# Retention and two gated products in one kernel: stores, roundings and word buffers in other places

## The chip, the cores and the metric

The kernel runs on one core of one Trainium2 chip. The core's engines are TensorE (PE, with its weight loads as PEld), VectorE (DVE), ScalarE (ACT), GpSimd (POOL) and SyncE (SP), which here issues nearly all transfers. The metric is the device time of one execution in microseconds, and the median of several runs is compared.

## The reference

A retention layer with a decaying state per head is followed by two two-layer networks, the first with x·sigmoid(x) between its layers, the second with a leaky maximum. All is fp32.

```python
for t in range(S):                                  # S = 768, B = 2, H = 8, D = 64
    state = gamma * state + einsum('bhd,bhe->bhde', k[:, :, t], v[:, :, t])
    y[:, :, t] = scale * einsum('bhd,bhde->bhe', q[:, :, t], state)
x = y as 1536 tokens x 512
h = x @ moe_w_in;  x = (h / (1 + exp(-h))) @ moe_w_out        # 512 -> 2048 -> 512
h = x @ moe2_w_in; return maximum(0.01 * h, h) @ moe2_w_out
```

## The kernel before

**Stages.** Attention works on 12 chunks of 128 tokens (`ORDER`), two at a time: masked scores, values, a running state. Each network then has an up phase (512 to 2048, 8 steps of two 128-feature blocks, class `Step`) and a down phase (2048 to 512). The network products multiply a rounded high part and a remainder of each operand in three fp32r terms (`TERMS`), so every operand is first split by `halves`: ACT writes the high part, DVE subtracts to give the low part. From the third step on, the up phase uses a seven-product scheme for 2x2 blocks (`product`, `rest`), with the products in the order 6, 2, 5, 7, 1, 4, 3 of a step (6, 2, 7, 5, 4, 3 in the last), where product 1 is the next step's.

**Order.** The order of work is written by hand, engine by engine, and each engine runs its own list in order. In the up phase `tasks[m]` lists what goes to the other engines ahead of product m. SP's list is one queue for loads and stores alike.

**Weights.** A weight tile w arrives as 64-bit words in one of two `ws` tiles (`load_w`). `words` (ACT, L144 and L146) takes a buffer from the list `rt` and reads the words into it and into `u`; `clamp` (DVE, L150 and L154), `signed` (L161) and `low` (L168) finish the value. `keep_w` stores it to memory as `scr` and puts the buffer at the end of `rt`; `fetch_w` takes a buffer from `rt` and loads it again. For tiles of the second network's down phase `keep_s` also forms four sums of blocks (L181) and stores them as `scrs`.

**Features.** `Step.act` applies the nonlinearity in place on the step's 128x3072 tile (two tiles `big` in turn), and `Step.keep` stores the tile, 1.5 MB, as `g` (L445). The down phase fetches `g` in pieces (`fetch_g` L459, `Two.load` L510) and splits them (`split_g`; `Two.high` L555 and `Two.left` L559). Steps 0 to 5 are stored in the step that follows; step 6 is stored after the whole last step (L952), then step 7 (L955).

**Down phase of the second network** (class `Two`). Units n = 0 to 7 multiply the first 512 tokens plainly (L586), units from 8 on use seven products for 256 tokens each (L602). Ahead of unit n stand the splits of the weights for n + 2 (`third`, L200 and L201) and of the features for n + 2. In units 1 to 8 the sums of weights, loaded by `ask` (L576) into one of two hold tiles (`sf`, `u`), are rounded into `S[k]` (L648, L654); only units from 8 on read `S`.

**Attention's last part.** `store_x(j)` takes chunk j's outcome: for j below 6 DVE multiplies it by a decay (L363) into `xf` or `tm`, then `halves` writes the operands of the first network; from 6 on `halves` reads PSUM and ACT copies the raw value (L371). Chunks 3, 4 and 5 (counted from 0) are the second half of the first 768 tokens; their operands are `b12[0]` (a slot `w`) and `xb[0]`. `first_t` and `rest_t` form differences of `xf` and `tm` in place on POOL, from 49.47 us on.

Of the kernel before, what the change touches and what calls it, by code (L numbers as in the profile page):

```python
# [18 lines left out]
C = 128  # L19
# [11 lines left out]
PER = N // C  # L31
Q = NF // 2
WARM = 18
LATE = 6
PLACES = 6
NCST = NP * C + C + H + H + NP

MIN_NORMAL = float(np.array(0x38000000, np.uint32).view(np.float32))
# [4 lines left out]
def retention_moe_kernel(ctx: ExitStack, tc: tile.TileContext, att, w1, w2, cst, out):  # L43
# [93 lines left out]
            s = (w1, w2)[layer][f, :, 512 * part:512 * part + 512]  # L137
            nc.sync.dma_start(out=t[:, n], in_=s.bitcast(I32).rearrange("p (n t) -> p n t", t=2))

    def words(w, which=(0, 1)):  # L140
        t = stage[w]
        if 0 in which:
            r = rs[w] = rt.pop(0)
            nc.scalar.activation(out=r.bitcast(F32), in_=t[:, :, :, 1].bitcast(F32), func=AF.Abs)  # L144
        if 1 in which:
            nc.scalar.activation(out=u, in_=t[:, :, :, 0].bitcast(U32), func=AF.Copy, scale=2.0 ** -29)  # L146

    def clamp(w):
        r = rs[w]
        nc.vector.tensor_scalar(  # L150
            out=r.bitcast(F32), in0=r.bitcast(F32), scalar1=MIN_NORMAL, scalar2=MAX_NORMAL,
            op0=ALU.max, op1=ALU.min,
        )
        nc.vector.tensor_scalar(  # L154
            out=r, in0=r, scalar1=3, scalar2=0x3FFFFFF8,
            op0=ALU.logical_shift_left, op1=ALU.bitwise_and,
        )
# [8 lines left out]
    def low(w):  # L166
        r = rs[w]
        nc.vector.tensor_tensor(out=r, in0=r, in1=u, op=ALU.add)  # L168
# [186 lines left out]
    def store_x(j):  # L355
        s, c = divmod(j, PER)
        a, b = c * C, c * C + C
        y = yu[j]
        g4 = lambda t: t.rearrange("p (a k i) -> p a k i", a=2, k=2)
        y = g4(y)  # L360
        f = (tm if s % 2 else xf)[s // 2][:, :, :, a:b]
        if j < LATE:
            nc.vector.tensor_tensor(out=f, in0=y, in1=g4(G), op=ALU.mult)  # L363
            y = f
        if s % 2 == 0:
            halves(*(xa[s // 2][:, n].rearrange("p (a k) n -> p a k n", a=2)[:, :, :, a:b] for n in range(2)), y)
        else:
            halves(*put(s, a, b, 0)[0:2], y[:, 0])
            halves(*put(s, a, b, 1)[0:2], y[:, 1])
        if j >= LATE:  # L370
            nc.scalar.activation(out=f, in_=y, func=AF.Copy)  # L371


    TERMS = ((0, 0), (0, 1), (1, 0))
# [118 lines left out]
    class Two:  # L493
# [67 lines left out]
        def run(self):  # L561
# [65 lines left out]
            def third(i):  # L627
                return split_2((1, 1, i), wt[(i - 2) // 3][:, (i - 2) % 3])

            for n in range(self.UNITS):  # L630
                s, i = divmod(n, Q)
                if i == 0 and s % 2:
                    y = lanes_of(0)[0] + [bank(2), bank(3)]
                elif i == 0:
                    y = lanes_of(1)[0] + [bank(0), bank(1)]
                if n + 4 < 10:
                    self.fetch(n + 4)
                if n + 2 < Q:
                    third(n + 2)
                if n + 4 < Q:  # L640
                    fetch_w((1, 1, n + 4))
                if n >= 4 and n + 6 < self.UNITS:
                    self.fetch(n + 6)
                if n + 2 < self.UNITS:
                    self.high(n + 2)
                if 1 <= n <= Q:
                    k = n - 1
                    nc.scalar.activation(out=S[k][0], in_=hold[k % 2], func=AF.Copy)  # L648
                if Q <= n + 3 < self.UNITS:
                    self.sums(n + 3)  # L650
                if n + 2 < self.UNITS:
                    self.left(n + 2)
                if 1 <= n <= Q:
                    nc.vector.tensor_tensor(out=S[k][1], in0=hold[k % 2], in1=S[k][0].bitcast(F32), op=ALU.subtract)  # L654
                for k in range(2) if n == 0 else [n + 1] if n + 1 < Q else []:
                    ask(k)
                if s == 0:
                    plain(n, i, y)
                    if i == Q - 1:
                        for c in range(4):  # L660
                            nc.scalar.activation(
                                out=o[:, 2 * c:2 * c + 2].rearrange("p b n -> p (b n)"), in_=y[c], func=AF.Copy
                            )
                            send(c)
                else:
                    seven(n, i, y)
                    if i == Q - 1:
                        finish(s + 1, y)

    with tc.manual_schedule():  # L670
# [48 lines left out]
        def load_next():  # L719
            w = next(asked, None)  # L720
            if w is not None:
                load_w(w)

        def signed(w):
            sign(w)
            load_next()
# [15 lines left out]
        def left_a():  # L742
# [6 lines left out]
        amid = {2: lambda: words(wa), 4: low_a}  # L749
        behind = {  # L750
            0: load_next, 2: lambda: clamp(wa), 3: lambda: signed(wa),
            4: lambda: (load_next(), clamp(wb)), 5: lambda: signed(wb),
        }
        places = [place(p) for p in range(2)]
        for j in range(0, NJ, 2):
# [41 lines left out]
        def up_tasks(layer, k):  # L797
            t = [[] for _ in range(8)]
            at = lambda n, *f: t[n].extend(f)
            if layer == 0 and k < 2:  # L800
                wd = first_w[3]
                if k == 0:
                    at(0, lambda: low(wb), lambda: first_t(0, nc.gpsimd), lambda: rest_t(0, nc.gpsimd))
                    at(1, lambda: words(wc), lambda: split_a(wb))
                    at(2, lambda: clamp(wc), lambda: signed(wc))
                    at(3, lambda: low(wc), lambda: sums(wc))
                    at(4, lambda: split_t(0, 0), lambda: first_t(1, nc.vector))
                    at(6, lambda: split_t(1, 0))
                else:
                    at(0, lambda: split_t(0, 1), lambda: rest_t(1, nc.vector))  # L810
                    at(2, lambda: split_a(wc), lambda: words(wd))
                    at(3, lambda: split_s(wc))
                    at(4, lambda: split_t(1, 1), lambda: clamp(wd))
                    at(5, lambda: signed(wd))
                    at(6, lambda: low(wd), lambda: sums(wd))
                return t
            if layer == 0:
                if k + 1 < Q:
                    a = first_w[k + 1]
                    at(0, lambda: split_a(a))  # L820
                    at(1, lambda: split_s(a))
                w = second_w[0][k - 2]
                if k + 2 < Q:
                    b = first_w[k + 2]
                    at(0, lambda: words(b, (0,)))
                    at(2, lambda: words(b, (1,)), lambda: clamp(b))
                    at(3, lambda: signed(b))
                    at(4, lambda: (low(b), sums(b)), lambda: words(w, (0,)))
                    at(5, lambda: words(w, (1,)), lambda: clamp(w))
                    at(6, lambda: (signed(w), low(w), keep_w(w)))  # L830
                else:
                    at(1, lambda: words(w))
                    if k + 1 < Q:
                        at(2, lambda: clamp(w))
                        at(3, lambda: signed(w))
                    else:
                        at(4, lambda: clamp(w), lambda: signed(w))
                    at(4, lambda: low(w))
                    at(5 if k + 1 < Q else 4, lambda: direct(w))
                return t  # L840
            w = second_w[1][k]
            n, m = (first_w[Q + k + d] if k + d < Q else None for d in (1, 2))
            if k == 0:
                at(0, lambda: fetch_w(n), lambda: first_t(1, nc.vector), lambda: rest_t(1, nc.gpsimd))
                at(1, lambda: split_t(1, 0))
                at(2, lambda: split_a(n))
                at(4, lambda: sums(n), lambda: fetch_w(m))
                at(6, lambda: split_s(n))
                at(7, lambda: split_t(1, 1), lambda: sums(m))
                return t  # L850
            if n:
                at(0, lambda: split_a(n))
                at(1, lambda: split_s(n))
            if m:
                at(1, lambda: fetch_w(m))
                at(4, lambda: sums(m))
            at(2, lambda: words(w))
            at(3, lambda: clamp(w))
            at(4, lambda: signed(w))
            at(5, lambda: (low(w), keep_s(w), direct(w) if k > 5 else keep_w(w)))  # L860
            return t
# [28 lines left out]
        def rest(s, n, before, tasks):  # L890
            seq = (6, 2, 5, 7, 1, 4, 3) if n else (6, 2, 7, 5, 4, 3)
            for m, p in enumerate(seq):
                if m == 2:
# [6 lines left out]
                    else:  # L900
                        Two.now.fetch(1)
                if m == 3:
                    s.act(0, 0)
                for t in tasks[m]:
                    t()
# [21 lines left out]
        for layer in range(2):  # L927
            steps = [Step(layer, i) for i in range(Q)] + [None]
            for k in range(Q):
# [19 lines left out]
                elif k == Q - 2:  # L949
                    tasks[4] += [lambda: fetch_g(0, 0, 0) if layer == 0 else Two.fetch_first()]  # L950
                rest(s, n, steps[k - 1], tasks)
            steps[Q - 2].keep()  # L952
            steps[Q - 1].act(0, 1)
            fetch_g(0, 0, 3) if layer == 0 else two_.fetch(3)
            steps[Q - 1].keep()  # L955
# [137 lines left out]
```

## Time and profile before

| | us |
|---|---|
| three runs: lowest, median, highest | 558.85, 560.48, 561.06 |
| profiled execution, whole | 561.33 |
| its span, first to last instruction | 559.5 |
| PE busy in it | 542.5 |
| DVE, ACT, POOL busy | 417.6, 301.8, 104.7 |

Times in the trace count from the span's start. Attention ends at about 51.5 us, the first network's up phase at 172.9, its down phase at 304.3; the second network's up phase ends at 426.0, and its plain units at 475. A wait is the idle time of an engine before an instruction, with what ended it in brackets. "PE busy" is modelled from the starts of pipelined matmuls, so what a wait costs is read from the starts of work before and behind it.

### The profile page before, as it was taken

How to read it: one execution, taken by the hardware profiler on the slowest of the kernel's cores; microseconds unless marked ns; L12 is line 12 of the kernel's file. 1: busy time of each engine (PE TensorE's matmuls, PEld its weight loads, DVE VectorE, ACT ScalarE, POOL GpSimd, SP SyncE). 2: the span in 40 equal slices, each digit the busy share in tenths (PEclk: the TensorE clock that was granted, in tenths of full speed). 3: DMA queues.
4: the chain of work that ended last, by engine and by line, in shares of the span. 5: the costliest groups of instructions: out<-in, count | busy, mean ns of one | idle time of the engine just before them, and what ended most of it. 6: DMA issues, size and time to landing. Idle time of an engine off the chain costs nothing.

```text
span 559.5 us, 8890 instructions
## 1 busy us (share of the span) xinstructions
PE 542.5 (97%) x3546; PEld 503.0 (90%) x3546; DVE 417.6 (75%) x546; ACT 301.8 (54%) x367; POOL 104.7 (19%) x92
## 2 busy tenths in 40 slices
PE   7989999999999999999999999998999979999996
PEld 6878999999998788888888999998999858999996
DVE  3798787999956687664867677767877278898993
ACT  2135586777774566644445376646765166443440
POOL 2585322333300000000600662202200000000000
PEclk8999999999999999999999999999999989999999
DMA  8982335778767977889274427776747986642521
GB/s 319 406 336 78 137 127 193 281 266 283 256 227 266 406 237 241 251 289 293 83 255 164 183 114 301 294 293 223 281 150 258 382 311 220 197 136 77 183 82 39
DMA packets 41789, 127.54 MB, mean 228 GB/s; under 512 B 3730, under 2 KB 12050, under 8 KB 39700
## 3 DMA queue, kind: packets, MB, share of 16 engines
q1 hardware_dynamic: 41456, 126.63, 63.8%
q8 instruction: 28, 0.46, 0.3%
q10 hardware_dynamic: 292, 0.34, 0.2%
q14 instruction: 13, 0.11, 0.1%
HBM read 85.01 MB, written 41.94 MB: 227 GB/s over the span
## 4 chain that ended last, share of the span: by engine, by line
PE 58%; DVE 17%; DMA 11%; ACT 5%; issue 5%; POOL 2%; SPq 1%; DVEq 0%; ACTq 0%; POOLq 0%
PE p L394 12%; PE b L394 9%; PE b L602 8%; PE p L471 6%; PE b L471 6%; PE p L602 6%; DMA scr<-r 4%; PE b L878 3%; DVE w L201 3%; DMA c<-g 2%; PE p L878 2%; PE p L586 2%; DVE r L168 2%; PE b L586 2%; DMA sf<-scrs 2%
## 5 line engine op out<-in xcount | busy, mean ns | idle before, releaser
L394 PE MATMUL p<-tt,w 128*128 128x384 f32 x468 | 87.9, 335 | 2.2 <-ACT c L426 2.2
L394 PEld LDWEIGHTS p<-tt,w 128*128 128x128 f32 x468 | 81.8, 188 | 2.9 <-ACT c L426 2.8
L471 PE MATMUL b<-w,wt 128*128 128x512 f32 x216 | 55.1, 390 | 0.5 <-DVE wt L201 0.5
L471 PE MATMUL p<-w,wt 128*128 128x512 f32 x216 | 54.8, 389 | 0.0
L201 DVE TENSOR_TENSOR w<-c,w 128x1024 fp32r<-128x1024 f32 x23 | 29.7, 1293 | 28.9 <-ACT w L200 28.9
L146 ACT ACTIVATE u<-ws 128x1024 int32<-128x1024 uint32 x32 | 36.5, 1139 | 26.3 <-DVE r L168 26.2
L426 ACT ACTIVATE c<-p 128x768 f32<-128x768 f32 x39 | 31.5, 811 | 32.4 <-PE p L394 27.1
L471 PEld LDWEIGHTS b<-w,wt 128*128 128x128 f32 x216 | 40.4, 188 | 9.4 <-DVE wt L201 1.1
L197 POOL TENSOR_TENSOR sf<-r 128x256 f32<-128x256 f32 x26 | 27.7, 1087 | 110.4 <-DVE r L168 59.8
L471 PEld LDWEIGHTS p<-w,wt 128*128 128x128 f32 x216 | 40.5, 188 | 8.4
L161 DVE SCALAR_TENSOR_TENSOR r<-ws,r 128x1024 int32<-128x1024 int32 x32 | 44.3, 1386 | 0.8
L144 ACT ACTIVATE r<-ws 128x1024 f32<-128x1024 f32 x32 | 36.5, 1140 | 13.6 <-DMA scr<-r 7.9
L430 DVE TENSOR_TENSOR big<-b,c 128x384 f32<-128x384 f32 x78 | 39.6, 550 | 5.0 <-ACT c L426 4.6
L168 DVE CUSTOM_DVE_ANT_0 r<-r,u 128x2048 uint16<-128x2048 uint16 x32 | 40.3, 1261 | 0.9
L200 ACT ACTIVATE w<-c 128x1024 fp32r<-128x1024 f32 x23 | 24.4, 1060 | 21.5 <-DMA c<-g 21.5
L201 DVE TENSOR_TENSOR w<-sf,w 128x1024 fp32r<-128x1024 f32 x14 | 17.1, 1225 | 23.3 <-ACT w L200 23.3
L154 DVE TENSOR_SCALAR r<-r 128x1024 int32<-128x1024 int32 x32 | 30.1, 940 | 1.1
L150 DVE TENSOR_SCALAR r<-r 128x1024 f32<-128x1024 f32 x32 | 24.7, 771 | 7.7 <-ACT r L144 7.7
L201 DVE TENSOR_TENSOR w<-r,w 128x768 fp32r<-128x768 f32 (+1 forms) x19 | 22.0, 1159 | 9.9 <-ACT w L200 9.9
L394 PE MATMUL b<-tt,w 128*128 128x384 f32 x156 | 29.2, 335 | 0.0
L394 PE MATMUL p<-xa,w 128*128 128x384 f32 x156 | 29.1, 335 | 0.0
L394 PE MATMUL b<-xb,w 128*128 128x384 f32 x156 | 29.1, 335 | 0.0
(178 smaller groups left out, 1129.7 us busy)
## 6 DMA issues: line engine op xcount, KB each, us to landing
ws<-w_dram SPq DMA_DIRECT2D x64, 512.0 KB, 5.5
g<-big SPq DMA_DIRECT2D x15, 1536.0 KB, 6.9
c<-g SPq DMA_DIRECT2D x30, 512.0 KB, 7.3
att_t<-att_dram SPq DMA_DIRECT2D x20, 512.0 KB, 8.6
scr<-r SPq DMA_DIRECT2D x18, 512.0 KB, 5.9
r<-scr SPq DMA_DIRECT2D x18, 512.0 KB, 5.8
c<-g SPq DMA_DIRECT2D x17, 256.0 KB, 3.4
scrs<-u SPq DMA_DIRECT2D x8, 512.0 KB, 4.0
```

Source lines behind the costliest of these rows:

```text
L144: nc.scalar.activation(out=r.bitcast(F32), in_=t[:, :, :, 1].bitcast(F32), func=AF.Abs)
L146: nc.scalar.activation(out=u, in_=t[:, :, :, 0].bitcast(U32), func=AF.Copy, scale=2.0 ** -29)
L154: nc.vector.tensor_scalar(out=r, in0=r, scalar1=3, scalar2=0x3FFFFFF8, op0=ALU.logical_shift_left, op1=ALU.bitwise_and,)
L161: nc.vector.scalar_tensor_tensor(out=r, in0=t[:, :, :, 1], scalar=-0x40000000, in1=r, op0=ALU.bitwise_and, op1=ALU.bitwise_or)
L168: nc.vector.tensor_tensor(out=r, in0=r, in1=u, op=ALU.add)
L201: nc.vector.tensor_tensor(out=l, in0=s, in1=h.bitcast(F32), op=ALU.subtract)
L394: nc.tensor.matmul(out=o, lhsT=a[:, ta, k * 128:k * 128 + 128], rhs=rhs(p, tb, k), start=(begin and m == 0), stop=(end and m == 5), skip_g ...
L426: nc.scalar.activation(out=ct[n][:, c, 0:N], in_=t[:, :, 0:N], func=AF.Copy)
L430: nc.vector.tensor_tensor(out=self.block(f, half, c), in0=t[:, :, 0:N], in1=ct[n][:, c, 0:N], op=ALU.add)
L471: nc.tensor.matmul(out=y, lhsT=l, rhs=r, start=(i == 0 and f == 0 and n == 0), stop=(i == Q - 1 and f == 1 and n == 2),)
L602: nc.tensor.matmul(out=y[at][:, 256 * half:256 * half + 256], lhsT=g[:, tg, b], rhs=w[:, tw, a] if sm is None else S[i][tw][:, sm], start= ...
L878: nc.tensor.matmul(out=y[m][0][p][:, 0:N], lhsT=a[:, ta, (A11, A21)[f] + kk // 2, k * 128:k * 128 + 128], rhs=x, start=(i == 0), stop=(i = ...
```

## The change

Five things are put elsewhere; no instruction is added or left out on any engine.

1. In the last step of each up phase, step 6 is stored ahead of the fourth of the last step's products and no longer behind all of them.
2. The sums of the second network's down weights are rounded in units 3 to 8 (`SUMS`) and asked for accordingly (`ASK`), where before each unit from 1 to 8 rounded one.
3. Chunks numbered 4 and 5 (the fifth and sixth of `ORDER`) are no longer rounded where their values are stored; `round_x` rounds them behind the fifth pair of chunks.
4. `words` takes the buffer that came back last from `rt`, in the up phase of the second network and for the down weights in that of the first.
5. In the second network's up phase one split of features (`split_t(1, 1)`) goes from the end of step 0 to the start of step 1.

```diff
-    def words(w, which=(0, 1)):
+    def words(w, which=(0, 1), at=0):
-            r = rs[w] = rt.pop(0)
+            r = rs[w] = rt.pop(at)
...
+LATER = (4, 5)
...  (store_x)
+        if j in LATER:
+            return
+        round_x(j, y)
...
-            4: lambda: (load_next(), clamp(wb)), 5: lambda: signed(wb),
+            4: lambda: (load_next(), [round_x(j) for j in LATER], clamp(wb)), 5: lambda: signed(wb),
...  (Two.run)
+            SUMS = {3: (0,), 4: (1,), 5: (2,), 6: (3, 4), 7: (5, 6), 8: (7,)}
+            ASK = {1: (0, 1), 3: (2,), 4: (3,), 5: (4,), 6: (5, 6), 7: (7,)}
...
-                if 1 <= n <= Q:
-                    k = n - 1
+                for k in SUMS.get(n, ()):
                     nc.scalar.activation(out=S[k][0], in_=hold[k % 2], func=AF.Copy)
...  (up_tasks)
-                    at(4, lambda: (low(b), sums(b)), lambda: words(w, (0,)))
+                    at(4, lambda: (low(b), sums(b)), lambda: words(w, (0,), -1))
...
-                at(7, lambda: split_t(1, 1), lambda: sums(m))
+                at(7, lambda: sums(m))
                 return t
+            if k == 1:
+                at(0, lambda: split_t(1, 1))
...
-            at(2, lambda: words(w))
+            at(2, lambda: words(w, at=-1))
...  (rest)
                 if m == 3:
+                    if not n:
+                        before.keep()
                     s.act(0, 0)
...
-            steps[Q - 2].keep()
             steps[Q - 1].act(0, 1)
```

SP's list at the end of the first network's up phase; `c<-g` are pieces of features for the down phase, `r<-scr` its weights, `ws` new words. Before:

```order
L459 DMA c<-g_1_968 128x2x512
L187 DMA r_73<-scr_1_2_1047 128x1024
L138 DMA ws_72<-w_dram 128x1024 x2
L459 DMA c<-g_2_1098 128x2x512
L187 DMA r_74<-scr_1_3_1177 128x1024
L445 DMA g_6_1678<-big_68 128x3072
L459 DMA c<-g_3_1228 128x2x512
L445 DMA g_7_1682<-big_69 128x3072
```

The same place in the changed kernel:

```order
L469 DMA c<-g_1_968 128x2x512
L188 DMA r_74<-scr_1_2_1047 128x1024
L455 DMA g_6_1621<-big_68 128x3072
L139 DMA ws_72<-w_dram 128x1024 x2
L469 DMA c<-g_2_1098 128x2x512
L188 DMA r_75<-scr_1_3_1177 128x1024
L469 DMA c<-g_3_1228 128x2x512
L455 DMA g_7_1682<-big_69 128x3072
```

The store of step 6 has moved ahead of the words, of the third piece of features and of the fourth weight tile. At the end of the second network's up phase it moves in the same way, ahead of one piece of features, one weight tile and one store of sums.

ACT's list in the first units of the second network's down phase; `wt<-r` is the high part of weights, `gh<-c` and `w_88<-c` that of features, `s` that of sums. Before:

```order
L200 ACTIVATE wt_3548<-r_75 128x1024
L555 ACTIVATE gh_3431<-c 128x1024
L648 ACTIVATE s_3550<-sf 128x1024
L200 ACTIVATE wt_3548<-r_73 128x1024
L555 ACTIVATE w_88<-c 128x1024
L648 ACTIVATE s_3550<-u 128x1024
```

The same place in the changed kernel:

```order
L201 ACTIVATE wt_3548<-r_2584 128x1024
L565 ACTIVATE gh_3431<-c 128x1024
L201 ACTIVATE wt_3548<-r_74 128x1024
L565 ACTIVATE w_88<-c 128x1024
L201 ACTIVATE wt_3549<-r_75 128x1024
L565 ACTIVATE gh_3563<-c 128x1024
L659 ACTIVATE s_3550<-sf 128x1024
```

The first rounding of sums has moved behind the operands of units 4 and 5; on DVE the low parts (L654) move with it.

DVE's list in attention, from the rounding of chunk 4 on; `big_69` holds the chunk's values, `c<-p` are masked scores. Before:

```order
L201 TENSOR_TENSOR w_86<-big_69,w_86 128x2x128
L201 TENSOR_TENSOR xb_66<-big_69,xb_66 128x2x128
L273 TENSOR_TENSOR c<-p_364,c 128x1024
L273 TENSOR_TENSOR c<-p_373,c 128x1024
L322 TENSOR_TENSOR gst<-gst,b_391 128x256 x2
L363 TENSOR_TENSOR big_69<-b_337,gst 128x2x2x128
L201 TENSOR_TENSOR w_86<-big_69,w_86 128x2x128
L201 TENSOR_TENSOR xb_66<-big_69,xb_66 128x2x128
L150 TENSOR_SCALAR r_73<-r_73 128x1024
```

Where they stand in the changed kernel, behind chunk 9 and ahead of the clamp of the next weights:

```order
L202 TENSOR_TENSOR w_87<-b_514,w_87 128x2x128
L202 TENSOR_TENSOR xb_67<-b_514,xb_67 128x2x128
L202 TENSOR_TENSOR w_86<-big_69,w_86 128x2x128
L202 TENSOR_TENSOR xb_66<-big_69,xb_66 128x2x128
L202 TENSOR_TENSOR w_86<-big_69,w_86 128x2x128
L202 TENSOR_TENSOR xb_66<-big_69,xb_66 128x2x128
L151 TENSOR_SCALAR r_74<-r_74 128x1024
L155 TENSOR_SCALAR r_74<-r_74 128x1024
L202 TENSOR_TENSOR w_87<-b_604,w_87 128x2x128
```

Four subtractions have left the stretch ahead of chunk 6's and chunk 8's masked scores and now stand ahead of the clamp and of chunks 10 and 11.

## Rows read from the trace of the kernel before

**Rows 1.** Waits of TensorE: who <- ended by: us in total, times, longest

```profile
PE b L283 <- DVE c L273: 2.2, 2, 1.8
PE p L394 <- ACT c L426: 2.2, 2, 1.7
PE p L586 <- ACT w L555: 2.1, 1, 2.1
```

**Rows 2.** Timeline of PE, units 2, 3 and 6: start, us, engine, line, operation

```profile
436.98 1.53 PE L586 MATMUL p<-wt,gh 128*128 128x512 f32 x6
...
442.48 1.53 PE L586 MATMUL p<-wt,gh 128*128 128x512 f32 x6
...
464.12 1.53 PE L586 MATMUL p<-wt,gh 128*128 128x512 f32 x6
```

**Rows 3.** Timeline of ACT there: the first rounding of sums

```profile
447.24 1.06 ACT L648 ACTIVATE s<-sf 128x1024 fp32r<-128x1024 f32 x1 [8.14 <-DMA sf<-scrs]
```

**Rows 4.** Timelines of SP and ACT; then a transfer issue with us to landing

```profile
422.69 0.52 SPq L510 DMA_DIRECT2D c<-g  x1
...
432.93 1.04 ACT L555 ACTIVATE gh<-c 128x1024 fp32r<-128x1024 f32 x1
...
434.47 2.04 SPq L187 DMA_DIRECT2D r<-scr  x1
...
r<-scr SPq DMA_DIRECT2D x1, 512.0 KB, 10.0
```

**Rows 5.** Stretches: PE, PEld, DVE, ACT, POOL busy; granted clock; DMA share; GB/s

```profile
38.40:41.80 3.40, 1.64 (x26) 1.43 (x28) 3.40 (x6) 1.08 (x2) 3.26 (x4) 1.00 0.34 134
...
451.50:454.90 3.40, 3.02 (x7) 2.44 (x8) 3.40 (x4) 2.55 (x3) 0.00 (x0) 0.50 0.87 286
```

**Rows 6.** Timeline of SP, end of the first network's up phase

```profile
169.59 0.59 SPq L187 DMA_DIRECT2D r<-scr  x1
...
173.43 0.53 SPq L459 DMA_DIRECT2D c<-g  x1
174.00 0.60 SPq L187 DMA_DIRECT2D r<-scr  x1
174.65 0.70 SPq L445 DMA_DIRECT2D g<-big  x1
```

**Rows 7.** Landings of the last three of these: KB, us from issue

```profile
c<-g SPq DMA_DIRECT2D x1, 512.0 KB, 6.9
...
r<-scr SPq DMA_DIRECT2D x1, 512.0 KB, 7.8
...
g<-big SPq DMA_DIRECT2D x1, 1536.0 KB, 10.9
```

**Rows 8.** Timelines of ACT, DVE and PE, units 2 and 3 of that down phase

```profile
180.41 1.06 ACT L200 ACTIVATE w<-c 128x1024 fp32r<-128x1024 f32 x1 [1.39 <-DMA c<-g]
...
182.65 1.22 DVE L201 TENSOR_TENSOR wt<-r,wt 128x1024 fp32r<-128x1024 f32 x1
...
183.80 1.52 PE L471 MATMUL b<-w,wt 128*128 128x512 f32 x6
...
190.38 1.19 PE L471 MATMUL b<-w,wt 128*128 128x512 f32 x4 [0.52 <-DVE wt L201]
```

**Rows 9.** Timelines of DVE, PE and PEld in attention and just behind it

```profile
29.14 0.43 DVE L201 TENSOR_TENSOR w<-big,w 128x256 fp32r<-128x256 f32 x1 [0.48 <-ACT w L200]
...
33.91 0.94 DVE L201 TENSOR_TENSOR w<-big,w 128x256 fp32r<-128x256 f32 x1 [0.48 <-ACT w L200]
...
40.08 1.09 PE L283 MATMUL b<-c,att_t 128*64 128x128 f32 x16 [1.81 <-DVE c L273]
...
51.87 2.22 DVE L154 TENSOR_SCALAR r<-r 128x1024 int32<-128x1024 int32 x1
...
58.22 0.99 PEld L878 LDWEIGHTS b<-w,w 128*128 128x128 f32 x6 [0.45 <-ACT big L371]
```

**Rows 10.** Waits of ACT: the words that wait for a store from their buffer

```profile
ACT r L144 <- DMA scr<-r: 7.9, 7, 3.8
```

More of the change, by code (lines that the diff above doesn't have):

```diff
@@ L364, in store_x, with round_x @@
             y = f
+        if j in LATER:
+            return
+        round_x(j, y)
+        if j >= LATE:
+            nc.scalar.activation(out=f, in_=y, func=AF.Copy)
+    def round_x(j, y=None):
+        s, c = divmod(j, PER)
+        a, b = c * C, c * C + C
+        if y is None:
+            y = (tm if s % 2 else xf)[s // 2][:, :, :, a:b]
         if s % 2 == 0:
@@ L369, in store_x @@
             halves(*put(s, a, b, 1)[0:2], y[:, 1])
-        if j >= LATE:
-            nc.scalar.activation(out=f, in_=y, func=AF.Copy)
     TERMS = ((0, 0), (0, 1), (1, 0))
@@ L652, in run @@
                     self.left(n + 2)
-                if 1 <= n <= Q:
+                for k in SUMS.get(n, ()):
                     nc.vector.tensor_tensor(out=S[k][1], in0=hold[k % 2], in1=S[k][0].bitcast(F32), op=ALU.subtract)
-                for k in range(2) if n == 0 else [n + 1] if n + 1 < Q else []:
+                for k in ASK.get(n, ()):
                     ask(k)
```

## The prediction

> **What bounds the kernel now.** I read the shares of busy time first: TensorE is busy for 542.5 of 559.5 us, so no other engine's total can be the bound, and what can be gained or lost is TensorE's waits. They stand in the waits of that engine [rows 1], and each is small; so I went to the timeline around each long one, looked at what the releasing engine had been doing, and then at the queue of transfers behind it. Three places matter. In attention PE waits once for 1.81 us for masked scores [rows 9]. In the second network's up phase it waits once for 1.7 us for a copy on ACT [rows 1]. In the second network's plain units it loses most: unit 3 starts 5.50 us behind unit 2, but unit 6 starts 21.64 us behind unit 3 [rows 2], where three units of 5.50 us are 16.50. That is 5.1 us lost at one place. The change touches all three, and it also touches a fourth, the start of the first network's down phase, where PE waits for only half a microsecond [rows 8].
>
> **The end of the second network (sums rounded later, step 6 stored sooner).** ACT stood idle for 8.14 us until the first sums landed, and rounded them from 447.24 on [rows 3]; the weights and features of unit 4 were queued behind that on ACT, and PE's first product of unit 4 waited 2.1 us for ACT [rows 1]. The weights had been there for some time: issued at 434.47, landed 10.0 us later, at 444.5 [rows 4]. Without the sums ahead of them ACT splits weights and features (1.04 us each [rows 4], or 1.06) from 444.5 to 446.6, DVE's two low parts (1.22 each, as in [rows 8]) follow to about 447.9, and unit 4 is due at 442.48 + 5.50 = 447.98. So even with the transfers as they are it just fits, and the earlier store takes its share of the queue out of their way: step 6's store takes 3.7 us of a full queue (worked out below from [rows 6, 7]), so the weights should land some 3 us sooner. I take the whole 5.1 us as gone. About 1.5 us of it is the clock: the stretch from 451.50 to 454.90 ran at a granted 0.50, the 1.2 GHz level [rows 5], after two pieces of idle time of 2.1 and some 1.1 us with a single product between them. The roundings come back in units 3 to 8, at most two in a unit beside two other splits: 4 x 1.22 = 4.9 us of DVE in 5.50 us. They fit, and what they feed is read from unit 8 on only. Bounds: -5.1, and -3.5 if one wait of 1.5 us takes its place.
>
> What the earlier store costs here: it goes ahead of a piece of features that was issued at 422.69 and landed within 4.3 us, at 427.0. With the 3.7 us it lands at 430.7, and ACT reads it at 432.93, since it is busy with the last step's work until then [rows 4]. 2.2 us are left, so I cost it at nothing; the rival below is that this cover isn't there.
>
> **The start of the first network's down phase (the same store).** Here the cover is missing. The third piece of features is issued at 173.43 and lands 6.9 us later, at 180.3; the next weights 174.00 + 7.8 = 181.8; the store of step 6, 174.65 + 10.9 = 185.5 [rows 6, 7]. They land in the order of issue, and the store takes 185.5 - 181.8 = 3.7 us by itself. In the change it is issued behind the weights of 169.59 [rows 6], so at about 170.2, and what was ahead of it, new words and this piece, comes 3.7 us later: the piece lands at 184.0. ACT waits for just that landing, starting at 180.41 [rows 8], and DVE finishes the low part of the weights of unit 2 at 182.65 + 1.22 = 183.9 [rows 8]. All that moves by 3.7 us, to 187.6. PE starts unit 2 at 183.80 [rows 8] and needs that low part by its third product, about 0.5 us on (six products take 1.5 us): some 0.4 us of slack, so unit 2 loses 3.3 us. Unit 3's wait at 190.38 (0.52 us [rows 8], 0.6 from start to start) is swallowed by it, as its features come behind the store in both orders and are no later. Net +2.7 us. Bounds: 0 if the loads don't have to wait for the store, +4.2 with a fall of the clock.
>
> The Trainium skill (DMA: Bandwidth & Descriptors, Queues, rings and completion order) says that completion isn't first in, first out for one issuing engine, since a later transfer may finish its writes ahead of an earlier one. By that the piece could land as before and the term would be zero, which is the first rival. The landings in [rows 7] follow the issues, so I price it by the rows.
>
> **Attention.** Four subtractions leave DVE ahead of chunk 8's masked scores: the two rows that are shown took 0.43 and 0.94 us, with 0.48 us of waiting for ACT ahead of each [rows 9], and their neighbours about as much. That is over 3 us of DVE, of which some 0.4 are lost again since the scores themselves are then late. PE's wait of 1.81 us [rows 9] goes, and with the smaller ones PE reaches the first network 2.5 us sooner. But the four come back, at 0.4 us each and with about 1 us of waiting for ACT (which first copies chunk 9), ahead of the clamp of the next weights (2.22 us beside POOL [rows 9]) and of chunks 10 and 11. POOL's differences now have to wait for chunk 5's rounding, since they overwrite its values, so the clamp runs beside them as before. Chunk 11 is thus finished when it was, within some tenths. PE needs its bank for the product that started at 58.22, behind ACT's last copy [rows 9]. So PE waits there for 2.8 us in place of 0.3, and nothing is gained: -0.1. Bounds -0.7 (a clamp less disturbed by POOL) to +2.0 (a fall of the clock, and half a microsecond).
>
> **Words and the split.** `words` waited seven times for a store from its buffer, 7.9 us in all, 3.8 the longest [rows 10]. With the buffer that was last split, no store is waited for. Only the longest reached PE, by the copy behind it (1.7 us [rows 1]). The other six average 0.7 us and cost PE nothing. A store that was slow in one execution made that wait, so I count -1.8 for the profiled execution and 0 for an ordinary one. The split of features moves by one place on ACT, behind an activation; its reader stands three products on. Nothing.
>
> **The sum.** Against the profiled execution's own 561.33: -5.1 + 2.7 - 0.1 - 1.8 = 557.0. That execution lies 0.85 us above the median of the three runs, and its slow store is not every run's, so on the median it is 560.48 - 5.1 + 2.7 - 0.1 = **558.0**, 0.4% less. About 0.5% (2.8 us) is what a measurement of this kernel can tell from no change, so I call this the same, close to the edge.
>
> **Rivals.** (a) The loads of the first network are not held by the store: 560.48 - 5.1 - 0.1 = 555.3. For it: the queue was idle ahead of 170 us; against it: the order of landings [rows 7]. (b) The clock falls at one of the new waits: the wait of unit 2 would be about 2.3 us, two products, then 1 us more, much like the one ahead of the slow stretch of [rows 5]. Against it, the single wait of 1.81 us in attention left the clock at 1.00 [rows 5, 9]. Price 1.5 us: 559.5. The Trainium skill (TensorE: Matmul & The Clock Gate, HAM oscillation) ties the fall to one gap without work beyond a certain length; by that no new wait would cost it, while the trace has a fall behind two shorter gaps. (c) Slower: the store holds the loads in the second network too. That decides if its piece of features lands over 2.2 us later than worked out; then unit 2 or 3 there waits by up to 3.3 us as in the first network, and with a fall of the clock at both places the time is 558.0 + 3.3 + 3.0 = 564.3. (d) The change doesn't do what it says: with the sums away ACT meets a late weight tile of units 4 to 6, and half of the 5.1 us stays: 560.5.
>
> **How the numbers follow.** Forecast 0.37, (a) 0.20, (b) 0.30, (c) 0.06, (d) 0.07. Faster by over 0.5% means under 557.7: all of (a), and somewhat under half of the forecast's own spread of about a microsecond, and a little of (b): 0.40. Slower means over 563.3: (c), 0.06. The rest, 0.54, is within. The range goes from just under (a), 555.0, to just over (d), 560.7; (c) and the tails are left out.
>
> **What would show it.** Unit 4 of the second network's plain units starts 5.5 us behind unit 3 and the granted clock stays at 1.00 there: the first term. In the first network's down phase ACT's split of the third piece starts near 184 in place of 180.4 and PE shows a wait of about 3 us in unit 2: the second. PE waits for 2 to 3 us ahead of the first network's product that needs chunk 11's bank, and none in attention: the third. I am wrong if unit 2 of the first network isn't late, or if a new wait stands in units 4 to 8 of the second.

## The result

The changed kernel takes **564.03 us** (median of 5 runs, 562.84 to 565.25) where the kernel before took 560.48 (558.85 to 561.88): a ratio of **1.0065**, 95% interval 1.0037 to 1.0093. It is slower by 3.6 us. The forecast was 558.0 in a range of 555.0 to 560.7, with a chance of 0.06 for a time over 563.3. The profiled execution took 563.52 us (span 561.7; before: 561.33 and 559.5).

The waits that the change was to remove are gone, and others stand in their place. TensorE's waits in the changed kernel (line, releasing engine and line; us in total, times, longest):

```profile
PE b L891 <- ACT big L370: 4.1, 1, 4.1
PE b L481 <- ACT wt L201: 3.1, 1, 3.1
PE p L404 <- ACT c L436: 1.2, 2, 0.6
...
PE b L481 <- DVE wt L202: 0.6, 1, 0.6
PE p L612 <- DVE w L569: 0.6, 1, 0.6
PE p L612 <- DVE gh L569: 0.5, 1, 0.5
PE b L284 <- DVE c L274: 0.4, 1, 0.4
```

Of the three rows of [rows 1] the wait for masked scores (1.8) is down to 0.4, that for ACT's `w` of unit 4 (2.1) is gone, and the longest wait for a copy on ACT is 0.6 where it was 1.7. The row of 4.1 is chunk 11's bank just behind attention, those of 3.1 and 0.6 on L481 are unit 2 of the first network's down phase, and the two on L612 are units 10 and 11 of the second network's down phase (each unit from 8 on has 21 products there, and the waits stand ahead of the 44th and the 65th; the expectations below call them units 8 and 9). And the granted clock falls behind the two long ones (columns as in [rows 5]):

```profile
58.30:61.60 3.30, 3.15 (x10) 3.16 (x11) 1.82 (x2) 2.49 (x4) 0.00 (x0) 0.50 0.41 146
191.40:194.70 3.30, 3.30 (x9) 2.63 (x8) 0.52 (x1) 3.30 (x4) 0.00 (x0) 0.50 0.99 394
448.00:458.00 10.00, 10.00 (x45) 8.23 (x45) 5.86 (x5) 5.37 (x6) 0.00 (x0) 1.00 1.03 401
```

The third stretch is where the kernel before had its 0.50 [rows 5]: there the clock stays at 1.00 and PE has no gap.

Both kernels issue the same 3546 products in the same order, so the start of each can be compared with its start before. PE's lag behind the kernel before, in the two profiled executions:

| place | lag, us | forecast of the step | measured step |
|---|---|---|---|
| the product that needs chunk 11's bank (58.22 before) | +0.2 | -0.1 | +0.2 |
| ten products on, behind the slow stretch | +1.7 | (none) | +1.5 |
| end of the first network's up phase | +2.5 | 0 | +0.8 |
| unit 3 of the first network's down phase | +7.7 | +2.7 | +5.2 |
| behind the copy that waited for words (380 before) | +5.8 | -1.8 | -1.9 |
| second network, behind unit 4 | +0.6 | -5.1 | -5.2 |
| end | +2.2 | 0 | +1.6 |

The 0.8 in the up phase stands behind one wait of PE, 0.54 us at 171.12, for a copy of ACT's; ahead of that copy ACT had waited 1.31 us for a load of features. Why that load came late isn't shown.

**Attention.** The four subtractions are gone from DVE ahead of the scores, and PE is 3.7 us ahead at 40 us. Then the clamp keeps DVE (start, us, engine, line, operation):

```profile
49.41 0.42 DVE L202 TENSOR_TENSOR xb<-big,xb 128x256 fp32r<-128x256 f32 x1
49.74 2.33 DVE L151 TENSOR_SCALAR r<-r 128x1024 f32<-128x1024 f32 x1
52.11 2.21 DVE L155 TENSOR_SCALAR r<-r 128x1024 int32<-128x1024 int32 x1
...
57.34 0.42 DVE L202 TENSOR_TENSOR xb<-b,xb 128x256 fp32r<-128x256 f32 x1 [0.45 <-ACT xb L201]
```

and PE waits for the bank that ACT copies out behind the last of these:

```profile
53.17 1.20 PE L891 MATMUL b<-xb,w 128*128 128x384 f32 x6
58.45 2.29 PE L891 MATMUL b<-w,w 128*128 128x384 f32 x6 [4.07 <-ACT big L370]
```

The six products of 58.45 take 2.29 us where those of 53.17 took 1.20: the 1.2 GHz level. Chunk 11 is finished when it was in the profiled execution before (58.22 against 58.45 for PE's product). The lead was 3.7 and not 2.5, since the kernel before had one more stretch at 0.50 in that execution, where this one has 1.00 (before, then after):

```profile
11.20:14.50 3.30, 3.30 (x50) 3.18 (x47) 1.16 (x1) 0.04 (x1) 1.73 (x2) 0.50 1.02 413
11.20:14.50 3.30, 3.30 (x75) 3.23 (x73) 1.26 (x2) 0.36 (x1) 1.72 (x2) 1.00 1.03 416
```

1.5 of the 3.7 us come from there; the lead goes entirely into the wait.

**The first network's down phase.** In the timeline of SP the store now goes out ahead of the last piece of features and of the next weights:

```profile
173.15 0.38 SPq L455 DMA_DIRECT2D g<-big  x1
...
176.98 0.90 SPq L469 DMA_DIRECT2D c<-g  x1
177.94 1.10 SPq L188 DMA_DIRECT2D r<-scr  x1
```

The same three issues with KB and us to landing:

```profile
g<-big SPq DMA_DIRECT2D x1, 1536.0 KB, 9.3
...
c<-g SPq DMA_DIRECT2D x1, 512.0 KB, 10.5
...
r<-scr SPq DMA_DIRECT2D x1, 512.0 KB, 10.9
```

ACT's roundings for unit 2 wait for the piece:

```profile
187.55 1.06 ACT L201 ACTIVATE w<-c 128x1024 fp32r<-128x1024 f32 x1 [5.65 <-DMA c<-g]
188.52 1.04 ACT L201 ACTIVATE wt<-r 128x1024 fp32r<-128x1024 f32 x1
```

and PE at the change from unit 1 to unit 2:

```profile
184.96 1.52 PE L481 MATMUL p<-w,w 128*128 128x512 f32 x6
189.61 0.81 PE L481 MATMUL b<-w,wt 128*128 128x512 f32 x2 [3.13 <-ACT wt L201]
191.06 1.42 PE L481 MATMUL b<-w,wt 128*128 128x512 f32 x3 [0.64 <-DVE wt L202]
```

The store lands at 173.15 + 9.3 = 182.4, the piece of features behind it at 176.98 + 10.5 = 187.5, in the order of issue. Before, the piece landed at 180.3 and PE began unit 2 at 183.80 [rows 7, 8]; now it begins at 189.61, with PE 2.5 us late already. That is 3.3 us of waiting; the second wait costs 1.0 from start to start, the slow stretch from 191.4 on 1.7, and 0.8 come back at unit 3, which no longer waits: 5.2 in all, 3.5 of it without the clock.

**The second network.** The firsts of units 2, 3, 4 and 6 among PE's products (against [rows 2]):

```profile
442.80 1.53 PE L596 MATMUL p<-wt,gh 128*128 128x512 f32 x6
...
448.29 1.54 PE L596 MATMUL p<-wt,gh 128*128 128x512 f32 x6
...
453.79 1.52 PE L596 MATMUL p<-wt,w 128*128 128x512 f32 x6
...
464.72 1.53 PE L596 MATMUL p<-wt,gh 128*128 128x512 f32 x6
```

5.50 us from unit 3 to unit 4, and 16.4 from unit 3 to unit 6, where it was 21.6. But the sums now meet the end of unit 7 (ACT):

```profile
476.47 1.06 ACT L659 ACTIVATE w<-sf 128x1024 fp32r<-128x1024 f32 x1 [1.77 <-DMA sf<-scrs]
477.43 1.06 ACT L672 ACTIVATE o<-p 128x512 f32<-128x512 f32 x2
...
479.34 0.97 ACT L565 ACTIVATE w<-r 128x896 fp32r<-128x896 f32 x1
```

ACT waits 1.77 us for a sum to land and only then copies the four results out and rounds the features of unit 10; PE waits for low parts of features in units 10 and 11, 0.6 and 0.5 us.

### The profile page after: what moved, and what is told of

Read it like the earlier page. It is cut to its first block, busy times and chain, and to the rows that moved or that the text cites. A ratio compares the mean times of both kernels' runs of the same rounds, so it can differ in the third digit from the quotient of the medians.

```text
span 561.7 us, 8870 instructions
## 1 busy us (share of the span) xinstructions
PE 543.6 (97%) x3546; PEld 504.4 (90%) x3546; DVE 415.8 (74%) x546; ACT 302.0 (54%) x367; POOL 103.2 (18%) x92
## 4 chain that ended last, share of the span: by engine, by line
PE 52%; DVE 23%; DMA 11%; ACT 6%; issue 5%; POOL 1%; SPq 0%; DVEq 0%; ACTq 0%; POOLq 0%
PE p L404 10%; PE b L404 7%; PE b L612 7%; PE p L481 7%; PE b L481 7%; PE p L612 6%; DVE r L169 3%; PE b L891 3%; DVE big L440 3%; DMA c<-g 3%; DVE r L155 3%; DMA r<-scr 3%; DVE w L202 2%; DVE r L162 2%; PE p L891 2%
## 5 line engine op out<-in xcount | busy, mean ns | idle before, releaser
L481 PE MATMUL b<-w,wt 128*128 128x512 f32 x216 | 55.9, 394 | 3.8 <-ACT wt L201 3.1
L481 PE MATMUL p<-w,wt 128*128 128x512 f32 x216 | 55.8, 394 | 0.0
L481 PEld LDWEIGHTS b<-w,wt 128*128 128x128 f32 x216 | 40.8, 189 | 13.0 <-ACT wt L201 3.5
L481 PEld LDWEIGHTS p<-w,wt 128*128 128x128 f32 x216 | 41.4, 192 | 8.7
L198 POOL TENSOR_TENSOR sf<-r 128x256 f32<-128x256 f32 x26 | 26.0, 1020 | 111.4 <-DVE r L169 61.9
L162 DVE SCALAR_TENSOR_TENSOR r<-ws,r 128x1024 int32<-128x1024 int32 x32 | 42.7, 1333 | 0.8
L155 DVE TENSOR_SCALAR r<-r 128x1024 int32<-128x1024 int32 x32 | 28.5, 891 | 1.1
L404 PE MATMUL b<-xa,w 128*128 128x384 f32 x156 | 29.1, 335 | 0.0
```

What stands on the lines that cost most here:

```text
L155: nc.vector.tensor_scalar(out=r, in0=r, scalar1=3, scalar2=0x3FFFFFF8, op0=ALU.logical_shift_left, op1=ALU.bitwise_and,)
L162: nc.vector.scalar_tensor_tensor(out=r, in0=t[:, :, :, 1], scalar=-0x40000000, in1=r, op0=ALU.bitwise_and, op1=ALU.bitwise_or)
L404: nc.tensor.matmul(out=o, lhsT=a[:, ta, k * 128:k * 128 + 128], rhs=rhs(p, tb, k), start=(begin and m == 0), stop=(end and m == 5), skip_g ...
L481: nc.tensor.matmul(out=y, lhsT=l, rhs=r, start=(i == 0 and f == 0 and n == 0), stop=(i == Q - 1 and f == 1 and n == 2),)
```

## Experiments

Each run is compared with the kernel before in the same set, so ratios to it are what compares across sets: its median was 560.35, 559.53 and 560.06 us in the three. The mean granted clock of a run is given beside its time where it tells something: the kernel before has 0.994 on the mean of 35 executions (0.987 to 0.998). The recorded expectations count chunks 5 and 6 from one: they are the chunks numbered 4 and 5 (`LATER = (4, 5)`). Chunks 8 to 11 are counted from nought everywhere.

**The changed kernel again** (`e5_changed_again`, no edit).

> The changed kernel itself, beside the others of this set: 564.0 by every theory.

562.96 us, 1.0057 (1.0032 to 1.0081), with the long waits where they were. Its mean granted clock is **0.989**. Taken over the span, and as if PE were busy through all of it, 1.1% of 561 us are 6.2 us lost to the lower level, against 0.6% of 558, 3.3 us, for the kernel before. So by this estimate 2.9 of the 3.4 us between the two are clock, and the waits themselves nearly cancel. Both figures are too high by about 1 us: the last 2.2 us of the span before and the last 1.7 after stand at 0.50 too, with PE already done. In the difference this nearly drops out.

**The waits filled.** In the changed kernel PE is kept busy in its two long waits, with products of zeros into a sum that is still open:

```
+ (the first network's first step, ahead of the last product of m == 2)
+   for _ in range(32):
+       nc.tensor.matmul(out=y[m][0][p][:, 0:256], lhsT=z[:, 0:128], rhs=z, start=False, stop=False, ...)
...
+ (its down phase, behind unit 1)
+   for _ in range(26):
+       nc.tensor.matmul(out=ys[3][:, 0:256], lhsT=z[:, 0:128], rhs=z, start=False, stop=False, ...)
```

> The changed kernel with its two long waits of PE filled: 32 products of zeros into an open sum ahead of the product that waits for chunk 11's bank, and 26 ahead of unit 2 of the first network's down phase. Both waits stay as long as they were, PE only isn't idle in them. Theory (the granted clock falls to 0.50 behind these two waits because PE was idle, and that costs 1.7 and 1.9 us on top of the waits): 564.0 - 3.6 = 560.4, and the granted clock is 1.00 from 15 to 555 us. Rival (the falls follow something else, or cost little): 564.0, or slower by what the fillers take too long.

560.16 us, 1.0023 (0.9997 to 1.0048): 2.8 us less than the changed kernel beside it, though chunk 11's bank comes when it did (58.45) and 58 products more are done. By the means of the twelve executions it is 2.1 us less (0.9 to 3.3): seven lie at 559.0 to 560.4 and five at 561.6 to 563.4. The mean clock is 0.997. The stretches of the two waits, and the one behind the second:

```profile
53.30:57.30 4.00, 4.00 (x36) 3.52 (x35) 2.20 (x4) 1.63 (x4) 3.92 (x3) 1.00 0.00 0
183.00:187.50 4.50, 4.31 (x33) 3.30 (x31) 1.24 (x2) 2.00 (x2) 0.00 (x0) 1.00 1.07 431
187.50:191.00 3.50, 2.86 (x12) 2.13 (x12) 1.13 (x1) 2.34 (x3) 0.00 (x0) 1.00 0.97 398
```

The falls hang on PE's being idle there, and without them the change can no longer be told from the kernel before. In the two traces PE's starts put 1.5 us of the gain behind chunk 11's wait and 1.7 behind that of unit 2; over many executions the division wasn't measured.

**The first network's store back** (`e1_store0_back`) and **the same store alone on the kernel before** (`e9_store0_alone`); the cut shows the first, the second makes the opposite move in the kernel before:

```
-                    if not n:
+                    if not n and s.layer:
                         before.keep()
...
+            if layer == 0:
+                steps[Q - 2].keep()
```

> The changed kernel with one part undone: in the first network the store of step 6 (1.5 MB) goes back to its old place behind the last step; in the second network it stays sooner. Theory (the store ahead of the loads makes unit 2 of the first network's down phase late): in the changed kernel PE waits there 3.29 and 0.89 us, and the granted clock falls right behind, so that PE is 5.3 us further behind the kernel before at unit 4 than ahead of unit 2; all of this goes: 564.0 - 5.3 = 558.7. Rival (the loads are late for some other reason, such as words and chunks that came late): the wait stays and the time is 564.0.

> The kernel before with one part of the change: the first network's store of step 6 goes out at the fourth product of the last step, the second network's stays. Theory (the loads are held by the store, 3.4 us of waits in unit 2 of the first network's down phase, and the granted clock falls behind them, 1.8): 5.2 us more than the kernel before of this set, some 565. Rival (the clock falls there only together with the other parts): 3.4 more, 563.4.

Back: 558.80 us, 0.9984 (0.9968 to 1.0000), and no wait for ACT in unit 2. Alone: 565.67, **1.0099** (1.0060 to 1.0138). In the second run PE waits in unit 2 as in the changed kernel:

```profile
PE b L471 <- ACT wt L200: 3.0, 1, 3.0
```

and the granted clock behind that wait is 0.50 (columns as before):

```profile
187.70:194.40 6.70, 6.16 (x15) 4.63 (x15) 3.52 (x4) 5.12 (x5) 0.00 (x0) 0.50 0.93 364
```

The store alone costs 5.6 us, in line with 3.5 of waits and about 2 of clock, and the theory holds from both sides. In this execution the slow stretch is twice as long as in the changed kernel's.

**Chunks 4 and 5 rounded in attention** (`e3_round_in_place`: `LATER = ()`).

> The changed kernel with one part undone: chunks 5 and 6 are rounded where they were before, inside attention. Theory (this part costs 2.4 us: PE's 3.7 us of lead is paid back with 3.9 of waiting, and the clock falls, 1.7, with some tenths): 561.6, with PE's wait of 1.8 us for masked scores back, and the granted clock at 1.00 there. Rival (the wait ahead of chunk 11 has another cause, such as the words' other buffer): the wait stays and the time is 564.0 or, with the wait for scores on top, 566.

559.47 us, 0.9999 (0.9982 to 1.0017); against 1.0057 that is 3.2 us, where 2.4 were expected, with some 1.7 us of uncertainty between the two. The wait for scores is back (waits of PE):

```profile
PE b L284 <- DVE c L274: 2.4, 2, 2.0
```

Ten of its twelve executions took under 561 us; the profiled one took 562.63, and in it the clock fell behind this wait as well:

```profile
38.40:41.70 3.30, 1.41 (x22) 1.20 (x24) 3.30 (x6) 1.08 (x2) 3.15 (x4) 1.00 0.36 140
41.80:45.00 3.20, 3.20 (x33) 2.87 (x31) 2.15 (x3) 0.60 (x1) 1.07 (x2) 0.50 0.03 4
```

That is the same wait that left the clock at 1.00 in the kernel before [rows 5, 9], 0.2 us longer: that it did nothing in one execution was no ground to expect nothing from a longer one.

Chunk 11's product also tells what the rounding costs. Two kept traces have the old rounding and, unlike the profiled execution before, no fall at 11 us: the store alone, and the run without both stores' move (`e10_no_stores`, below). They start that product here:

```profile
57.18 1.34 PE L878 MATMUL b<-w,w 128*128 128x384 f32 x6
...
56.99 1.32 PE L891 MATMUL b<-w,w 128*128 128x384 f32 x6
```

Against these two, 58.45 is 1.3 and 1.5 us late, and not 0.2. So the profiled execution before hid a cost of the later rounding.

**The clamp behind chunks 10 and 11** (`e2_clamp_behind`), and that with the store back (`e4_store0_clamp`):

```
-  4: lambda: (load_next(), [round_x(j) for j in LATER], clamp(wb)), 5: lambda: signed(wb),
+  4: lambda: (load_next(), [round_x(j) for j in LATER]), 5: lambda: (clamp(wb), signed(wb)),
```

> The changed kernel with one order turned round in attention: DVE (and ACT) finish chunks 10 and 11 ahead of the clamp of the next weights, not behind it. Theory (the clamp, 2.33 and 2.21 us of DVE beside POOL, is what keeps the bank of chunk 11 from PE now that PE comes earlier): the wait of 4.07 us goes, the fall of the clock behind it too (1.7 us): 564.0 - 5.8 = 558.2. Rival (DVE has as much to do either way, so that the later clamp makes the words of the next weights late and PE waits for those instead): 562 to 564, with a new wait of PE at 60 to 75 us.

> The first two together: the store of step 6 back in the first network, and the clamp behind chunks 10 and 11. If both terms are as read from the trace and add up: 564.0 - 5.3 - 5.8 = 552.9, faster than the kernel before by 7.6 us. Rival (what PE gains in attention it loses later, since the transfers of the first network don't come sooner): 556 to 558.

560.69 us, 1.0017 (0.9999 to 1.0035), and 556.07, 0.9934 (0.9913 to 0.9954). The wait for chunk 11 is gone in both and no fall follows there, but each is some 3 us above what was expected (by ratio). In the second PE is 3.8 us ahead of the kernel before at chunk 11's product and only 0.7 at 83 us, behind two waits for ACT's copies; the longer one in PE's timeline:

```profile
82.63 2.39 PE L404 MATMUL p<-xa,w 128*128 128x384 f32 x12 [2.21 <-ACT big L449]
```

DVE reaches the first step's features only behind the clamp and the sign of the next weights, beside POOL (DVE of the same run):

```profile
54.24 2.23 DVE L155 TENSOR_SCALAR r<-r 128x1024 int32<-128x1024 int32 x1
56.50 2.75 DVE L162 SCALAR_TENSOR_TENSOR r<-ws,r 128x1024 int32<-128x1024 int32 x1
...
64.57 0.69 DVE L155 TENSOR_SCALAR r<-r 128x1024 int32<-128x1024 int32 x1
65.30 1.23 DVE L162 SCALAR_TENSOR_TENSOR r<-ws,r 128x1024 int32<-128x1024 int32 x1
```

(the same two lines take 0.69 and 1.23 us once POOL is quiet). So the rival holds in part: the lead that attention yields is mostly paid back in the first two steps of the network, one wait or another. But these waits are shorter than the one of 4.07, and with the store back the mean clock is 0.999.

**The sums alone** (`e7_sums_alone`: the kernel before with the tables of units for roundings and requests).

> The kernel before with one part of the change: the sums' roundings in units 3 to 8, the stores where they were. Theory (the 5.1 us in unit 4 are due to the rounding on ACT alone, and the transfers just fit): 560.4 - 5.0, and 1.2 back for the new short waits in units 8 and 9: 556.6. Rival (without the sooner store the weights of unit 4 are too late, so that this part gains only together with the store): 558.5 to 560.4, with PE waiting for weights ahead of unit 4.

556.90 us, **0.9948** (0.9924 to 0.9972). No wait ahead of unit 4; its first products of units 3, 4 and 6:

```profile
442.06 1.54 PE L586 MATMUL p<-wt,gh 128*128 128x512 f32 x6
...
447.55 1.52 PE L586 MATMUL p<-wt,w 128*128 128x512 f32 x6
...
458.48 1.53 PE L586 MATMUL p<-wt,gh 128*128 128x512 f32 x6
```

16.4 us again. The rival (the sooner store is needed) falls.

**Without both stores' move** (`e10_no_stores`: as the changed kernel, both stores at their old places, chunks 4 and 5 in attention) and **with the second network's alone** (`e8_store0_round`).

> The changed kernel with the order of both stores undone and chunks 5 and 6 rounded in attention; left of the change are the sums in units 3 to 8, the words and the split. Theory (the sums don't need the sooner store in the second network either): as the sums alone, 0.5% less than the kernel before, 556.9, or up to 0.6 better by the words. Rival (the sooner store in the second network brings the half a microsecond or more by which the version with it was ahead of the sums alone): 557.5 or more, and a wait ahead of unit 4.

> The changed kernel with two parts undone: the first network's store at its old place, and chunks 5 and 6 rounded inside attention. Theory (both parts cost what the runs showed, 5 us and 4, and the rest of the change gains): 554.5 to 555.5, and no later than the kernel with the clamp behind chunks 10 and 11, 556.1. Rival (the parts overlap: what is gained at one is taken by a wait at the other): 558 to 559.

556.36, 0.9932 (0.9910 to 0.9954), and 556.10, 0.9932 (0.9905 to 0.9958), the second 0.6 above the top of what was expected. The sooner store of the second network makes no difference that can be measured, and nor do words and split, beside 0.9948 for the sums alone; each could hide up to some 2 us.

With these, four kernels differ only in two parts, the rounding of chunks 4 and 5 and the first network's store (ratios to the kernel before):

| | rounded in attention | rounded later |
|---|---|---|
| store of step 6 where it was | 0.9932 (`e8`) | 0.9984 (`e1`) |
| stored sooner | 0.9999 (`e3`) | 1.0057 (`e5`), 1.0065 (result) |

In medians the later rounding costs 2.9 us, the sooner store 3.8, and the rest of the change brings 3.8, each with an interval of some 1.5 to 1.8 us to either side; the three add up to within 1 us of what was measured. The sum of the prediction had -0.1, +2.7 and -5.1. With the clamp behind chunks 10 and 11 (`e4`, 0.9934) the later rounding no longer costs anything that can be told, but it doesn't gain on 0.9932 either.

**The sums spread** (`e11_sums_spread`, on top of store and clamp) and **one chunk later** (`e12_one_chunk`: that with `LATER = (5,)`).

```
-  SUMS = {3: (0,), 4: (1,), 5: (2,), 6: (3, 4), 7: (5, 6), 8: (7,)}
+  SUMS = {3: (0,), 4: (1,), 5: (2,), 6: (3, 4), 7: (5,), 8: (6,), 9: (7,)}
```

> The first network's store back, the clamp behind chunks 10 and 11, and the last three sums rounded in units 7, 8 and 9 (one each) in place of two in unit 7 and one in unit 8. Theory (in the changed kernel ACT waits for a sum to land in unit 7, and so reaches the copies of the results, and behind them the features of unit 10, 2 us late; that makes PE's waits of 0.7 and 0.6 us in units 8 and 9): these waits go, 556.1 - 1.3 = 554.8. Rival (DVE has more to do there than it can, whichever unit takes the roundings): 556.1, with the waits one unit later.

> As the run with the sums spread, but only chunk 6 is rounded later, chunk 5 in attention. Theory (the lead of PE in attention is paid back in the first step of the network anyway, since ACT and DVE have the same work by then; half of the moved work brings as much as all of it): within 0.5 us of the run with the sums spread, with a shorter wait of PE near 80 us and some wait for scores near 38. Rival (each rounding that leaves attention is a gain): 1 us slower than that run.

**555.11 us, 0.9918** (0.9886 to 0.9950), the fastest of all, 5.0 us under the kernel before. None of PE's waits names line 612 any more; ACT copies the results as soon as PE has them and rounds the late sum behind the features:

```profile
466.17 1.09 ACT L672 ACTIVATE o<-p 128x512 f32<-128x512 f32 x2 [0.64 <-PE p L596]
...
468.09 0.97 ACT L565 ACTIVATE w<-r 128x896 fp32r<-128x896 f32 x1
468.93 1.08 ACT L659 ACTIVATE w<-sf 128x1024 fp32r<-128x1024 f32 x1
```

In the trace the cause of those waits is shown; in the time the gain of 1 us lies inside the intervals. One chunk: 556.07, 0.9926 (0.9897 to 0.9955), not to be told from the former, with the wait of 2.2 us near 80 us unchanged, where the theory had a shorter one. In its profiled execution the clock fell behind that wait:

```profile
83.30:86.70 3.40, 3.40 (x13) 3.40 (x12) 3.30 (x5) 0.63 (x2) 0.00 (x0) 0.50 0.00 0
```

In the runs `e2`, `e4` and `e11` the same wait of 2.2 us left the clock at 1.00. This comparison decides nothing on the rounding.

## Why the prediction was wrong

- **The clock is the step that failed.** The sum put a fall of the clock at the two new waits at nothing. It stood in rival (b) alone, "The clock falls at one of the new waits", 0.30, with a price of 1.5 us and one place. The clock fell at both, 1.5 us in attention and 1.7 in unit 2, and over many executions the changed kernel loses an estimated 2.9 us more to it than the kernel before; with the waits filled 2.8 us come back. The argument against, that "the single wait of 1.81 us in attention left the clock at 1.00", compared a wait of 1.81 with forecast waits of 2.8, and of 2.3 with another of 1 close behind; a wait of 2.0 in the same place brought the fall. The bounds had room for a fall at each place (+2.0 in attention, where 1.7 was measured, and +4.2 in the down phase, where it was 5.2), but the sum took neither, and the range took one. With both bounds the sum is 558.0 + 2.1 + 1.5 = 561.6, still 2.4 us under the result.
- **The Trainium skill's rule** (TensorE: Matmul & The Clock Gate, HAM oscillation) ties a fall to one gap beyond a certain length, and by it no wait of the size forecast would have cost the clock. The fall behind 4.07 us agrees with it. But the traces also show a fall behind a single wait of 2.01 us, another behind one of 2.23, and one behind 3.13 with 0.64. The measurement decides; the prediction's likeliest case had come out on the side of the rule.
- **The store in the first network: right in mechanism, undersized.** +2.7 was forecast without the clock, 3.5 was measured. The piece landed 7.1 us later than before, 4.6 against PE, and not 3.7: the store took 3.9, and the weights ahead of it, issued at 172.47, landed at 178.5, 1.5 us later against PE than before. Why they did is open. The second wait came on top. Rival (a), that the loads aren't held, falls by the landings. Of the rule that the prediction cited there from the Trainium skill (DMA: Bandwidth & Descriptors, Queues, rings and completion order), no run here shows an instance: the 203 transfers of SP with a landing in the trace landed in the order of issue in both kernels.
- **Attention: the number is right in part by luck.** The place was named rightly, and in the pair of profiled executions the net is +0.2 for a forecast of -0.1. But the forecast and this comparison both rest on one execution of the kernel before, which had the slow stretch at 11 us. "Chunk 11 is thus finished when it was, within some tenths" doesn't hold against executions without it: there it is 1.3 to 1.5 us late, ahead of the clock's 1.5, and in medians the part costs 2.9. What was not seen is that the clamp alone stood between DVE and chunk 11, and that the wait would reach 4.1.
- **The second network: right in mechanism.** -5.2 in the profiled execution for -5.1. The guess that it fits even without the sooner store holds too, and rival (c) doesn't occur. But "They fit" was wrong for unit 7: the busy time fits, the landing of a sum ahead of the copies doesn't, and it cost 1.6 us in units 10 and 11. Over many executions the sums alone bring 2.9 us (interval 1.5 to 4.3), with the new waits in it, where one execution with its slow stretch promised 5.1.
- **Words: right.** -1.9 against the profiled execution, nothing that can be told in the median.
- **The medians.** Between the profiled executions the change costs 2.2 us and between the medians 3.6: before's profiled execution lay 0.85 above its median and had the slow words (1.8), after's lies 0.5 below.

Between the profiled executions the sum was -4.3 (557.0 - 561.33) and PE ended 2.2 late, 6.5 us apart: 3.2 by the clock at two places, 0.8 by the store's size, 1.6 by units 10 and 11, 0.8 in the first network's up phase, and the rest in small ones. In medians the forecast of 558.0 lacks 6 us, and there the table of four kernels divides it: 3.0 at the rounding, 1.1 at the store, 1.3 at the rest of the change, and some tenths where the two parts meet.

## What to carry to other kernels

Price a wait of TensorE with the fall of the clock that can come behind it: here several short waits gave way to two long ones, most of the loss of 3.4 us was clock, and filling the two waits with harmless products gave 2.8 back. A store of 1.5 MB put sooner into a full queue delayed the loads behind it by its own 3.7 to 3.9 us, so ask at each place where the same code runs whether the cover is there; here one call site had it and the other hadn't. A rounding that has to wait for a landing must not stand ahead of work that is due. And a term read against one profiled execution takes over that execution's luck: look at the same place in a second trace.

## What was not expected of the hardware

- The clock's answer to a wait isn't the same in every execution: the wait for scores, 1.81 us in one trace, 2.01 in another, left the clock at 1.00 in the first and not in the second. One of 2.2 us near 82 us was followed by a fall in one trace of four, and one of 0.8 to 1.4 us at 11 us, which all 14 traces have, in four. The mean granted clock of the kernel before ranges from 0.987 to 0.998. What decides it stays open.
- The slow stretch behind the same wait of 2.9 to 3.1 us lasted from 191.4 to 194.7 in one execution of the changed kernel, and twice as long (187.7 to 194.4) in the run with the store alone. The kernel alone doesn't decide that: in the repeat of the changed kernel (`e5_changed_again`) it was as long (the stretch in full):

```profile
189.20:195.90 6.70, 5.75 (x13) 4.13 (x14) 3.52 (x4) 5.11 (x6) 0.00 (x0) 0.50 1.03 416
```
